# Attention and a gated MLP on one core: shared tile as column tiles, V loaded a group ahead, four scaled-activation buffers, a wider spread of the second batch's transposes, and later padding copies

## The chip, the cores and the metric

The kernel runs on one core of a Trainium2 chip. The metric is the device time of one execution in microseconds (us). Most numbers below come from one profiled execution of each kernel. TensorE is called PE, VectorE DVE, ScalarE ACT, GpSimd POOL and SyncE SP in the profile; SP and POOL issue most of the DMAs.

One measure of my own is used throughout. The kernel has a set-up and then nine feed-forward groups. **Groups** means the time from the start of the first feed-forward matmul (bank<-UT,W) to the end of the last VectorE instruction, and a group's length is the time between two such starts, read from the timeline.

## The reference

```python
# attention: B=8, H=8, S=576, D=64; window 32, 8 global positions
scores = scale * q @ k.T ; masked outside the window except global rows/columns
attn = softmax(scores) ; x = (attn @ v) as (B, S, 512)
# gated MLP over tokens, then channels
a1 = alpha1 * x + beta1
u  = x + lam * einsum('ts,bsd->btd', w_tok, a1)          # token mix, 576 x 576
a2 = alpha2 * u + beta2
out = u + lam * (relu(a2 @ w_ch1) @ w_ch2)               # 512 -> 2048 -> 512
```

## The kernel before

Each batch of 576 tokens is four tiles of 128 tokens and 64 left over; two batches share one tile for their leftovers ("S"). The feed-forward runs over nine groups of four tiles. While group g runs on PE, the attention of batch g+1, its token mix, and the loads of batch g+2 are woven in between by slot number (128 feed-forward matmuls make 128 slots). The program issues every engine's work in the order of the slots, so a slot number also fixes who stands behind whom in each queue.

```python
def finish_u(t, ps):                       # after a token-mix tile
    nc.vector.tensor_tensor(out=x, in0=ps, in1=x, op=ALU.add)           # DVE add, frees the bank
    ...
    ub = UB[nub[0] % 2]                    # two buffers
    nc.gpsimd.tensor_tensor(out=ub, in0=x, in1=A2, op=ALU.mult)         # POOL, 1.28 us
    nc.sync.dma_start_transpose(out=UT[g % 2][:, :, js], in_=ub)        # SP, UT feeds the next group

def tok_shared(p):                         # shared tile: 2 x 5 matmuls 128x512
    # par 0: columns 64:192 of wtT, par 1: columns 0:128; 64 of the 128 columns are zeros
    ...
def tr_pair(b, hp):                        # first two batches: transposes on PE
    ring = tr0_ps if b == 0 else sc_ps     # second batch: the two score banks
    ...
for g in range(9):                         # group g; nb = g + 2
    timed(prefetch(nb), slots, 1, 50)      # K, Q and V of batch nb
    timed(xbars(nb), slots, 44, 78)        # DMA transposes of K and Q; V's shifted copy
    timed([qpad(hp) ...] + [gcols(nb)], slots, 86, 104)   # DVE: padded copy QP<-QT
    ...                                    # gathered rows' transposes (KGT) at slots 56 and 60
    parts = [(attention(g + 1), 2, 83), (token_mix(g + 1), 97, 115 if g < 3 else 122)]
```

The softmax here doesn't subtract the row's maximum and nothing guards it: scores larger than these inputs give would overflow.

## Time and profile before

| | before |
|---|---|
| median of 3 runs | 419.55 us |
| profiled span | 418.4 us |
| first group starts at | 56.85 us |
| groups | 358.28 us |
| PE busy | 91% |

The head of the page (busy time, share of the span, instructions), the slice rows of PE and of its granted clock, and the chain that ended last:

```profile
PE 382.3 (91%) x3071; PEld 213.9 (51%) x3071; DVE 235.1 (56%) x621; ACT 168.3 (40%) x318; POOL 213.3 (51%) x285
PE   0658888998999989989999999999999999999996
PEclk9996899999999999999999999999999999999999
PE 65%; DVE 13%; DMA 11%; POOL 4%; issue 3%; ACT 2%; SPq 1%; DVEq 0%; POOLq 0%; ACTq 0%
```

PE is the limit, but not everywhere: the first five slices (52 us) are set-up, and later slices that are not 9 hold waits. The view of waits names them (who waited for whom; us in total, times, longest):

```profile
PE bank L117 <- DVE QP L567: 1.9, 2, 1.0
PE bank L117 <- DMA UT<-UB: 1.6, 2, 1.2
PE bank L117 <- POOL XL L397: 1.3, 1, 1.3
PE bank L117 <- DVE KGT L241: 1.2, 2, 0.9
PE bank L117 <- DVE XR L410: 1.2, 1, 1.2
...
PE bank L117 <- issue: 0.6, 1, 0.6
...
POOL UB L425 <- DMA UT<-UB: 11.1, 9, 2.3
...
DVE QP L214 <- issue: 4.4, 2, 2.8
```

The 0.6 us under "issue" are the wait at the start of the second group. A displayed wait is about 0.15 us shorter than the lost time, since the end of the matmul before it is modelled (that same wait is 0.72 us by the starts of the matmuls); from the starts of all matmuls the holes after the first group's start sum to 11.4 us. L117 is the line of the helper that issues nearly all matmuls, so tile names and not lines tell them apart.

### The profile page before, as it was taken

To read this page: it belongs to the slowest core of one execution; us is meant where nothing else is said; L and a number is where in the kernel's file an instruction comes from. 1 tells how busy PE (TensorE), PEld (TensorE's weight loads), DVE (VectorE), ACT (ScalarE), POOL (GpSimd) and SP (SyncE) were. 2 spreads that over 40 slices of the span, in tenths; PEclk is the share of its full clock that TensorE was granted. 3 is DMA by queue.
4 is the path that set the end of the run, shared out by engine and by line. 5 is a ranking of instruction groups with operands and counts; after the bars stand their busy time and mean duration, and the time that the engine had idled before them with its cause. 6 is when DMAs were issued, how large, how long until landed. Compare 5 with 4: busy or idle time off the path is not lost.

```text
span 418.4 us, 8079 instructions
## 1 busy us (share of the span) xinstructions
PE 382.3 (91%) x3071; PEld 213.9 (51%) x3071; DVE 235.1 (56%) x621; ACT 168.3 (40%) x318; POOL 213.3 (51%) x285
## 2 busy tenths in 40 slices
PE   0658888998999989989999999999999999999996
PEld 0538545653465446535664565456645654444443
DVE  3765495587355946586459556845577555104013
ACT  2545236810484057303840483038405820450720
POOL 8635938435865389427853797369514335100000
PEclk9996899999999999999999999999999999999999
DMA  8999999991999179946994499549963002201002
GB/s 179 246 239 223 115 178 112 144 121 50 132 155 150 64 120 128 146 101 102 164 144 111 102 137 145 119 92 152 137 132 101 0 15 76 75 2 75 25 27 76
DMA packets 161691, 48.26 MB, mean 115 GB/s; under 512 B 147530, under 2 KB 154770, under 8 KB 161652
## 3 DMA queue, kind: packets, MB, share of 16 engines
q0 software_dynamic: 98752, 16.99, 62.0%
q1 hardware_dynamic: 62100, 30.36, 38.8%
q8 instruction: 24, 0.39, 0.4%
q10 hardware_dynamic: 800, 0.39, 0.4%
q14 instruction: 15, 0.12, 0.1%
HBM read 39.28 MB, written 9.44 MB: 116 GB/s over the span
## 4 chain that ended last, share of the span: by engine, by line
PE 65%; DVE 13%; DMA 11%; POOL 4%; issue 3%; ACT 2%; SPq 1%; DVEq 0%; POOLq 0%; ACTq 0%
PE bank L117 64%; DMA XR<-in_q_dram 4%; DVE QP L214 3%; DMA Kb<-in_k_dram 2%; DMA QT<-Qb 2%; DVE QP L567 1%; DMA UT<-UB 1%; DMA SR<-in_k_dram 1%; DVE XR L507 1%; DVE OT L506 1%; POOL UB L425 1%; DVE XR L410 1%; DVE XR L353 1%; POOL XL L371 1%; ACT E L293 1%
## 5 line engine op out<-in xcount | busy, mean ns | idle before, releaser
L117 PE MATMUL bank<-UT,W 128*128 128x512 bf16 x576 | 159.8, 379 | 3.0 <-DMA UT<-UB 1.6
L117 PE MATMUL bank<-W,HT 128*128 128x512 bf16 (+2 forms) x592 | 140.4, 373 | 0.0
L491 ACT ACTIVATE HT<-bank,bias 128x512 bf16<-128x512 f32 x144 | 99.0, 687 | 68.3 <-PE bank L117 67.5
L293 ACT ACTIVATE E<-bank 128x416 f16<-128x416 f32 (+1 forms) x96 | 47.5, 514 | 130.7 <-PE bank L117 129.2
L117 PEld LDWEIGHTS <-HT 128*128 128x128 bf16 x592 | 53.7, 98 | 53.5 <-issue 0.4
L117 PEld LDWEIGHTS <-W 128*128 128x128 bf16 x640 | 50.2, 97 | 28.8 <-issue 3.7
L371 POOL TENSOR_TENSOR XL<-XR,LA 128x384 bf16<-128x384 f32 x32 | 32.3, 1010 | 63.2 <-DVE XR L353 38.3
L425 POOL TENSOR_TENSOR UB<-XR,A 128x512 bf16<-128x512 f32 x28 | 35.9, 1286 | 49.0 <-DVE XR L410 21.4
L506 DVE TENSOR_TENSOR OT<-bank,LAM 128x512 f32<-128x512 f32 (+2 forms) x37 | 24.9, 672 | 53.5 <-PE bank L117 53.3
L117 PE MATMUL bank<-XL,wtT 128*128 128x512 bf16 x180 | 46.8, 389 | 3.2 <-POOL XL L397 1.3
L117 PE MATMUL bank<-RG,G 128*128 128x65 f16 x320 | 44.4, 196 | 4.7 <-DVE RG L321 3.5
L117 PEld LDWEIGHTS <-PT 128*128 128x128 f16 x576 | 34.0, 100 | 21.6 <-issue 5.4
L117 PE MATMUL bank<-Ve,PT 128*128 128x65 f16 x320 | 44.5, 197 | 0.0
L117 PE MATMUL bank<-QP,KT 128*128 128x144 bf16 (+1 forms) x288 | 33.9, 232 | 6.2 <-ACT E L293 4.0
L117 PEld LDWEIGHTS <-G 128*128 128x128 f16 x320 | 31.6, 99 | 15.0 <-DVE G L248 0.2
L117 PEld LDWEIGHTS <-KT 128*128 128x128 bf16 x288 | 25.2, 102 | 23.6 <-issue 7.2
L117 PE MATMUL bank<-Vo,PT 128*128 128x65 f16 x256 | 36.1, 195 | 0.0
L198 POOL DMA_DIRECT2D Ve<-in_v_dram x40 | 34.4, 869 | 2.2 <-PE bank L117 0.9
L300 DVE TENSOR_TENSOR PGQ<-E,gqm 128x80 f16<-128x80 f16 x64 | 11.1, 215 | 36.7 <-ACT E L293 36.7
L117 PEld LDWEIGHTS <-wtT 128*128 128x128 bf16 x180 | 17.9, 99 | 23.9 <-issue 4.2
L353 DVE TENSOR_TENSOR XR<-bank,rd 128x384 f32<-128x384 f32 x64 | 27.2, 424 | 2.3
L507 DVE TENSOR_TENSOR XR<-OT,XR 128x512 f32<-128x512 f32 (+2 forms) x33 | 26.7, 810 | 1.6
(130 smaller groups left out, 413.1 us busy)
## 6 DMA issues: line engine op xcount, KB each, us to landing
out_dram<-XR SPq DMA_DIRECT2D x31, 256.0 KB, 2.3
W<-in_moe_w_ch_dram POOLq DMA_DIRECT2D x4, 1024.0 KB, 19.0
Vo<-Ve SPq DMA_DIRECT2D x14, 260.0 KB, 3.5
Ve<-in_v_dram POOLq DMA_DIRECT2D x24, 128.0 KB, 10.0
Kb<-in_k_dram POOLq DMA_DIRECT2D x24, 128.0 KB, 6.0
Qb<-in_q_dram POOLq DMA_DIRECT2D x24, 128.0 KB, 6.7
Ve<-in_v_dram POOLq DMA_DIRECT2D x16, 96.0 KB, 8.9
XR<-in_k_dram SPq DMA_DIRECT2D x3, 512.0 KB, 15.2
```

The lines of the kernel that those rows point to most:

```text
L117: nc.tensor.matmul(out=o, lhsT=l, rhs=r, start=st, stop=sp, skip_group_check=True)
L198: nc.gpsimd.dma_start(out=Ve[b % 2][r0 : r0 + hi - lo, c, :, 0:D], in_=v[b, :, lo:hi, :].rearrange("h p d -> p h d"))
L214: nc.vector.tensor_copy(out=QP[r, hp, a, :, 0:64], in_=QT[r, hp, 0:S].rearrange("p (t j) -> p t j", j=64))
L293: nc.scalar.activation(out=e[:, UOFF[u] : UOFF[u + 1]], in_=ps[:, 0:off], func=AF.Exp, bias=0.0, scale=0.125)
L300: nc.vector.tensor_tensor(out=pg[:, :, c0 : c0 + 16].rearrange("p c (a g) -> p c a g", a=2), in0=gq_in, in1=gq_m, op=ALU.mult)
L353: nc.vector.tensor_tensor(out=xo, in0=pv[:, :, :, 0:64], in1=rb, op=ALU.mult)
L371: xl_eng(b).tensor_tensor(out=XL[b % 2][:, 0:3, 128 * hp : 128 * hp + 128], in0=xo, in1=bass.AP(l.tensor, l.offset, [l.ap[0], [0, 3], [1, ...
L410: nc.vector.tensor_tensor(out=x, in0=ps, in1=x, op=ALU.add)
L425: nc.gpsimd.tensor_tensor(out=ub, in0=x, in1=A2, op=ALU.mult)
L491: nc.scalar.activation(out=HT[:, ec, :], in_=st["ps"], func=AF.Relu, bias=bias1[:, ec : ec + 1], scale=1.0)
L506: nc.vector.tensor_tensor(out=ot, in0=ps, in1=LAM[:, lo:hi], op=ALU.mult)
L507: nc.vector.tensor_tensor(out=x, in0=ot, in1=x, op=ALU.add)
```

## The change

Its intent: fewer PE slots for the shared tile, and fewer waits of PE at the second batch's transposes, at group starts and behind VectorE. The core of the diff (layout changes of wtT and set-up fills cut):

```diff
-    UB = [T(f"UB{i}", [P, DM], BF16) for i in range(2)]
+    UBt = T("UB", [P, 4, DM], BF16)
+    UB = [UBt[:, i, :] for i in range(4)]
...
     def tok_shared(p):
-        (two halves of five full-width matmuls)
+        def f():
+            ps = pv_ps()
+            for s in range(5):
+                for par in range(2):
+                    l = wt4o[:, 0:64] if s == 4 and par == 1 else wtT[:, s, 0:64]
+                    mm(ps[64 * par : 64 * par + 64, :], l, XL4[par] if s == 4 else XL[par][:, s, :], s == 0, s == 4)
+            finish_u(("S", p), ps)
...
-            ring = tr0_ps if b == 0 else sc_ps
+            ring = tr0_ps if b == 0 else pv_ps
...                                          (and their order among the scores)
-            timed(prefetch(nb), slots, 1, 50)                     # K, Q, V
+            timed(prefetch(nb), slots, 1, 34)                     # K, Q (first group: 1, 42, with V)
-            timed(xbars(nb), slots, 44, 78)
+            timed(xbars(nb), slots, 44, 75); V's copy at slot 78
-                slots[56], slots[60]: gathered rows' transposes
+                slots[84 if g else 98], slots[87 if g else 100]
-            timed([qpad...] + [gcols], slots, 86, 104)
+            timed([qpad...] + [gcols], slots, 89 if g else 101, 105 if g else 122)
+            timed(prefetch_v(nb + 1), slots, 85 if g else 122, 96 if g else 127)
-            parts = [(first_attention(1), 4, 98), (token_mix(1), 106, 120)]
+            parts = [(first_attention(1), 4, 94), (token_mix(1), 106, 119)]
```

More of the change, by code (lines that the diff above doesn't have):

```diff
@@ L153 @@
     W2 = T("W2", [P, 16, DM], BF16)
-    wtT = T("wtT", [P, 5, 704], BF16)
-    wt4o = T("wt4o", [P, 704], BF16)
+    wtT = T("wtT", [P, 5, S], BF16)
+    wt4o = T("wt4o", [P, S], BF16)
     mask = T("mask", [P, NW, 64], FP16)
@@ L182 @@
     TST = SR[:, 1, :]
-    WTB = HTt[:, 0 : 5 * 640].rearrange("p (c s) -> p c s", c=5)
+    WTB = HTt[:, 0 : 5 * S].rearrange("p (c s) -> p c s", c=5)
     def xs(t):
@@ L422, in finish_u @@
             return
-        ub = UB[nub[0] % 2]
+        ub = UB[nub[0] % 4]
         nub[0] += 1
@@ L432, in f @@
             ps = pv_ps()
-            cs = slice(192 + 128 * i, 320 + 128 * i)
+            cs = slice(64 + 128 * i, 192 + 128 * i)
             for s in range(4):
@@ L441, in tok_shared @@
     def tok_shared(p):
-        st = {}
-        def half(par):
-            def f():
-                if par == 0:
-                    st["ps"] = pv_ps()
-                ps = st["ps"]
-                cs = slice(64, 192) if par == 0 else slice(0, 128)
-                for s in range(4):
-                    mm(ps, wtT[:, s, cs], XL[par][:, s, :], par == 0 and s == 0, False)
-                mm(ps, wtT[:, 4, cs] if par == 0 else wt4o[:, cs], XL4[par], False, par == 1)
-                if par == 1:
-                    finish_u(("S", p), ps)
-            return (1.1, f)
-        return [half(0), half(1)]
+        def f():
[5 more added lines that the diff above has]
+            finish_u(("S", p), ps)
+        return [(1.1, f)]
     def gap(w):
@@ L527 @@
     OT = [OTt[:, 0:DM], OTt[:, DM : 2 * DM]]
-    LB = T("LB", [P, DM], FP32)
+    LB = UBt[:, 2:4, :].rearrange("p a b -> p (a b)").bitcast(FP32)
     def fill(ap, val=0.0, eng=None):
@@ L644 @@
     fill(Ve[0][:, :, :, 64:65], 1.0, g_)
-    fill(WTB[:, :, S:640], 0.0, g_)
-    fill(WTB[64:128, 4, :].bitcast(FP32), 0.0, g_)
     for hp in range(HP):
@@ L680 @@
     fill(G[:, :, 640:704], 0.0, g_)
-    fill(wtT[:, :, 0:64], 0.0, g_)
     fill(wt4o[0:64, :].bitcast(FP32), 0.0, g_)
-    fill(wt4o[64:128, 0:64], 0.0, g_)
+    fill(wtT[64:128, 4, :].bitcast(FP32), 0.0, g_)
     fill(ones, 1.0, g_)
@@ L730, in wtok_tr @@
         ps = mlp_ps().bitcast(BF16)
-        cols = slice(128 * k, 128 * k + 128) if k < 5 else slice(448, 576)
-        for n, tcn in enumerate((4, 0, 1, 2, 3)):
-            nc.tensor.transpose(out=ps[:, 128 * n : 128 * n + 128], in_=WTB[:, tcn, cols], identity=identb)
+        c0, n = (128 * k, 128 if k < 4 else 64) if k < 5 else (448, 128)
+        cols = slice(c0, c0 + n)
+        nc.tensor.transpose(out=ps[0:n, 0:64], in_=WTB[0:64, 4, cols], identity=identb[0:64, 0:64])
+        for t in range(4):
+            nc.tensor.transpose(out=ps[0:n, 64 + 128 * t : 192 + 128 * t], in_=WTB[:, t, cols], identity=identb)
         if k < 5:
-            nc.scalar.copy(out=wtT[:, k, 64:704], in_=ps[:, 0:640])
+            nc.scalar.copy(out=wtT[0:n, k, :], in_=ps[0:n, 0:S])
         else:
-            nc.scalar.copy(out=wt4o[64:128, 64:704], in_=ps[64:128, 0:640])
+            nc.scalar.copy(out=wt4o[64:128, :], in_=ps[64:128, 0:S])
     def run(*items):
@@ L780 @@
     for sc_ in range(5):
-        mm(psr, ones, wtT[:, sc_, 192:704], sc_ == 0, sc_ == 4)
+        mm(psr, ones, wtT[:, sc_, 64:576], sc_ == 0, sc_ == 4)
     for sc_ in range(5):
-        mm(psr2[:, 0:64], ones, wtT[:, sc_, 64:128], sc_ == 0, sc_ == 4)
-    nc.scalar.copy(out=wtT[64:65, 4, 192:704], in_=psr[64:65, :])
-    nc.scalar.copy(out=wtT[64:65, 4, 64:128], in_=psr2[64:65, 0:64])
-    nc.scalar.copy(out=wt4o[0:1, 192:704], in_=psr[0:1, :])
-    nc.scalar.copy(out=wt4o[0:1, 64:128], in_=psr2[0:1, 0:64])
+        mm(psr2[:, 0:64], ones, wtT[:, sc_, 0:64], sc_ == 0, sc_ == 4)
+    nc.scalar.copy(out=wtT[64:65, 4, 64:576], in_=psr[64:65, :])
+    nc.scalar.copy(out=wtT[64:65, 4, 0:64], in_=psr2[64:65, 0:64])
+    nc.scalar.copy(out=wt4o[0:1, 64:576], in_=psr[0:1, :])
+    nc.scalar.copy(out=wt4o[0:1, 0:64], in_=psr2[0:1, 0:64])
     psb = mlp_ps()
@@ L810, in first_attention @@
         w = [pv_x(b, hp) + pv_y(b, hp) for hp in range(HP)]
-        a = [t_[0], tr_tail(b), gap(0.3), g[0], t_[1], gap(0.3), g[1], gap(0.3)] + s[0] + [t_[2], gap(0.3), g[2], s[1][0], s[1][1], t_[3], gap(0.3), g[3], s[1][2], gap(0.5)]
+        a = [t_[0], tr_tail(b), gap(0.5), t_[1], g[0], gap(0.5), g[1], gap(0.3), s[0][0], t_[2], gap(0.3), s[0][1], g[2], s[0][2], t_[3], gap(0.3)]
+        a += [s[1][0], g[3], s[1][1], s[1][2], gap(0.4)]
         a += [gk_all(b, pv_ps), gap(0.5), q_[0], gap(0.6), s[2][0], s[2][1]] + w[0] + [q_[1], s[2][2], s[3][0], s[3][1]] + w[1] + [q_[2], s[3][2], gap(0.9)]
@@ L821, in prefetch, with prefetch_v @@
             a.append(lambda c=c: load_kq_std(q, Qb, b, c))
-        for c in range(5):
-            a.append(lambda c=c: load_v(b, c))
-        return a
+        return a
+    def prefetch_v(b):
+        return [lambda c=c: load_v(b, c) for c in range(5)]
     def xbars(b):
@@ L830, in xbars @@
             a.append(lambda c=c: xbar_q(b, c))
-        a.append(lambda: copy_vo(b))
         return a
@@ L848 @@
         if nb < NB:
+            if g == 0:
+                timed(prefetch(nb) + prefetch_v(nb), slots, 1, 42)
+            else:
+                timed(prefetch(nb), slots, 1, 34)
+            timed(xbars(nb), slots, 44, 75)
+            slots[78].append(lambda: copy_vo(nb))
             if nb % 2 == 0:
                 pr = nb // 2
-                slots[1].append(lambda pr=pr: gather(pr))
+                slots[1].insert(0, lambda pr=pr: gather(pr))
                 slots[44] += [lambda: gather_x(0), lambda: gather_x(1)]
-                slots[56].append(lambda pr=pr: gather_tr(pr, 0))
-                slots[60].append(lambda pr=pr: gather_tr(pr, 1))
-            timed(prefetch(nb), slots, 1, 50)
-            timed(xbars(nb), slots, 44, 78)
-            timed([lambda hp=hp: qpad(hp) for hp in range(HP)] + [lambda: gcols(nb)], slots, 86, 104)
+                slots[84 if g else 98].append(lambda pr=pr: gather_tr(pr, 0))
+                slots[87 if g else 100].append(lambda pr=pr: gather_tr(pr, 1))
+            timed([lambda hp=hp: qpad(hp) for hp in range(HP)] + [lambda: gcols(nb)], slots, 89 if g else 101, 105 if g else 122)
+            if nb + 1 < NB:
+                timed(prefetch_v(nb + 1), slots, 85 if g else 122, 96 if g else 127)
         def wrap(i):
```

## The prediction

> **What bounds it now.** The page's engine table has TensorE (PE) busy 91% of a 418.4 us span; no other engine passes 56%, and the chain of waits gives PE 65%. The slice row shows two regimes: set-up until about 57 us, with PE fed slowly by DMA, VectorE and ScalarE, then nine groups in which PE is nearly full. From 57 us only two things can shorten the run: fewer PE slots, or fewer holes between them. I listed the starts of all matmuls in the PE timeline (a 128x512 one starts every 0.2145 us) and summed what exceeds that pace after 57 us: about 11 us, in few places:
>
> - 60 to 70 us, second batch's transposes: 3.3 us (VectorE copies of QP, then ScalarE's exponential)
> - 96 to 98 us: 1.8 us (POOL's XL, behind VectorE's QP padding)
> - group starts at 109, 150, 234 us: 0.7, 1.4, 0.6 us (UB to UT)
> - 171 and 255 us: 0.5 and 1.0 us (copy of the gathered transposes, KGT)
> - 184 us: 1.3 us (VectorE held until the QT transposes landed)
>
> **What the change does.**
>
> 1. Column tiles. A shared tile is ten 128x512 matmuls, 2.15 us. It becomes five pairs whose 64-column halves use different array columns. The Trainium skill, "TensorE: Matmul & The Clock Gate", Part 3, says such matmuls run concurrently; "TensorEngine Tiling (Array Packing)", Key Properties and Restrictions, says that a change of mode drains the array and that column tiling has no fast weight load. No pair is in this trace. I expect 1.3 to 1.4 us instead of 2.15: 0.75 us, four times, 3 us, all on PE's path.
> 2. Second batch's transposes in three PV banks, interleaved with scores: removes the wait for two score banks. But VectorE has about 9.8 us of copies and masks in a stretch where PE has 7.4 us, so not all goes: 2 us of 3.3.
> 3. First group: QP padding after the last norms. The 1.8 us hole goes, but padding now meets the token-mix adds (0.69 us each) and output adds; VectorE is near full from slot 93 on, so the wait at the next group start grows. Net 1.3 us.
> 4. V a group ahead: a third of the loads leaves the stretch where K/Q loads and QT/KT transposes (7.8 us to landing) run. The VectorE wait for QT (2.8 us) and the 184 us hole go: 1.2 us.
> 5. Four UB: POOL's 11.1 us of waits on UT<-UB mostly vanish; on PE's path 1 us at group starts.
> 6. Gather transposes later: 1.5 us at 171 and 255.
> 7. Set-up: fewer fills (0.9 us POOL), shorter copies of wtT: at most 0.3 us on the path.
>
> Sum about 10 us, less some 2 us for new waits: V loads just before the token mix may slow UT landings (2.5 us median, 6.0 at worst), and VectorE queues.
>
> **Prediction.** 411.3 us, range 407.8 to 415.0; faster by over 2%: 0.47; within 2%: 0.51; slower: 0.02.
>
> **What would show it.** Shared-tile matmuls start in pairs a few ns apart, five pairs in about 1.1 us plus switches; gk in the first group starts about 2 us earlier relative to the group's start; no PE wait on KGT; PE waits on UT<-UB under 1 us in total; POOL's wait on UT<-UB below 3 us; no VectorE wait for QT; PE holes after 57 us about 4 us instead of 11.
>
> **What would make it wrong.** The tiles do not overlap (weight loads serialise them): 3 us lost. VectorE is so full between 60 and 70 us, or at the end of the first group, that holes only move. V traffic delays UT, so that each group start gains a wait. All good together would give about 407.

## The result, and the profile after

The changed kernel took 406.65 us at the median (405.53 to 408.16, 4 runs) beside 419.52 us for the kernel before; the ratio is 0.9698 (95% interval 0.9657 to 0.9739). Ratios here are the mean time of one kernel's fast runs over that of the other's of the same rounds, so not quite the ratio of the medians. 406.65 lies 1.2 us under the stated range, and the gain of 12.9 us is more than one and a half times the 8.2 us predicted.

The same parts of the page, after:

```profile
PE 375.4 (93%) x3071; PEld 210.2 (52%) x3071; DVE 230.0 (57%) x621; ACT 167.2 (41%) x318; POOL 210.5 (52%) x282
PE   0657889999899999999999999999999999999996
PEclk9998999999999999999999999999999999999999
PE 87%; DVE 6%; POOL 2%; DMA 1%; issue 1%; ACT 1%; SPq 0%; DVEq 0%; POOLq 0%
```

Its waits, those of PE from the first group's start on (the view of waits with a window from 54.8 us): of the first five PE lines shown of before only two small rests stand, both on QP; line numbers moved by a few.

```profile
PE bank L117 <- issue: 1.1, 1, 1.1
...
PE bank L556 <- DVE QP L560: 0.4, 1, 0.4
PE bank L117 <- DVE QP L560: 0.3, 1, 0.3
...
POOL UB L426 <- DMA UT<-UB: 0.3, 1, 0.3
```

The 1.1 us under "issue" are the wait at the start of the second group, for UT. VectorE no longer waits for QT at all. The profiled spans are 418.4 and 403.6 us, 14.8 us apart. They split into groups (358.28 to 345.91, 12.37 us), first group's start (56.85 to 54.87, 1.98 us) and the end after the last VectorE instruction (3.28 to 2.87 us, 0.41 us, which no run here explains). The 1.98 us cannot be put down to the change: over the profiles of all twenty kernels below the first group starts anywhere from 54.65 to 57.61 us, and the kernel before with small additions is found at 54.93, 56.19 and 56.58. So the groups are what has to be explained. Their lengths, in us:

| group | 1 | 2 | 3 | 4 | 5 | 6 | 7 | 8 | 9 | sum |
|---|---|---|---|---|---|---|---|---|---|---|
| before | 52.37 | 40.98 | 43.82 | 40.17 | 42.99 | 39.89 | 41.76 | 27.63 | 28.66 | 358.28 |
| after | 47.63 | 39.61 | 41.13 | 39.61 | 41.13 | 39.61 | 40.91 | 27.63 | 28.65 | 345.91 |

The shared tile itself, in the PE timeline of the kernel before (start us, us, engine, line, operation, operands, array shape, count); its ten matmuls are the rows on XL:

```profile
103.54 1.24 PE L117 MATMUL bank<-XL,wtT 128*128 128x512 bf16 x5
104.62 0.59 PE L117 MATMUL bank<-W,HT 128*128 128x512 bf16 x2
105.05 1.03 PE L117 MATMUL bank<-XL,wtT 128*128 128x512 bf16 x4
105.92 0.38 PE L117 MATMUL bank<-XL,wt4o 128*128 128x512 bf16 x1
```

and after:

```profile
96.68 0.81 PE L117 MATMUL bank<-W,HT 128*128 128x512 bf16 x3
97.42 1.27 PE L117 MATMUL bank<-XL,wtT 128*64 128x512 bf16 x9
98.31 0.38 PE L117 MATMUL bank<-XL,wt4o 128*64 128x512 bf16 x1
98.62 0.60 PE L117 MATMUL bank<-W,HT 128*128 128x512 bf16 x2
```

Ten full-width matmuls take ten slots of 0.2157 us. The column tiles take 1.20 us from the first start (97.42) to the next ordinary matmul (98.62), and 0.1 us more on the way in: the third of the matmuls at 96.68 starts at 97.11, so 0.31 us pass and not 0.2157. A tile thus costs 1.3 in place of 2.16 us and saves 0.86 us.

### The profile page after: what moved, and what is told of

Read it like the earlier page. It is cut to its first block, busy times and chain, and to the rows that moved or that the text cites. A ratio compares the mean times of both kernels' runs of the same rounds, so it can differ in the third digit from the quotient of the medians.

```text
span 403.6 us, 8090 instructions
## 1 busy us (share of the span) xinstructions
PE 375.4 (93%) x3071; PEld 210.2 (52%) x3071; DVE 230.0 (57%) x621; ACT 167.2 (41%) x318; POOL 210.5 (52%) x282
## 4 chain that ended last, share of the span: by engine, by line
PE 87%; DVE 6%; POOL 2%; DMA 1%; issue 1%; ACT 1%; SPq 0%; DVEq 0%; POOLq 0%
PE bank L117 86%; DMA SR<-in_k_dram 1%; DVE QP L560 1%; POOL XL L372 1%; PE bank L556 0%; POOL Ve L199 0%; PE bank L418 0%; DVE PT L306 0%; DVE OT L539 0%; POOL XL L717 0%; DVE PT L525 0%; ACT QP L560 0%; DVE QP L576 0%; DVE Kb L539 0%; ACT E L294 0%
## 5 line engine op out<-in xcount | busy, mean ns | idle before, releaser
L117 PE MATMUL bank<-XL,wtT 128*128 128x512 bf16 (+1 forms) x180 | 41.2, 380 | 0.5 <-POOL XL L372 0.5
L301 DVE TENSOR_TENSOR PGQ<-E,gqm 128x80 f16<-128x80 f16 x64 | 10.2, 201 | 34.5 <-ACT E L294 32.7
L192 POOL DMA_DIRECT2D Kb<-in_k_dram x30 | 26.8, 894 | 0.1
```

The source lines that it names most:

```text
L117: nc.tensor.matmul(out=o, lhsT=l, rhs=r, start=st, stop=sp, skip_group_check=True)
L192: nc.gpsimd.dma_start(out=dst[0:n, c, :].rearrange("p (h d) -> p h d", d=D), in_=src[b, :, c * P : c * P + n, :].rearrange("h p d -> p h d"))
L301: nc.vector.tensor_tensor(out=pg[:, :, c0 : c0 + 16].rearrange("p c (a g) -> p c a g", a=2), in0=gq_in, in1=gq_m, op=ALU.mult)
```

## The experiments

Eighteen kernels ran; each was timed beside the kernel before on the same chip. Labels with a_ start from the changed kernel, those with b_ from the kernel before.

### Is a column tile fast because two run side by side?

a_unpaired:

```diff
-            for s in range(5):
-                for par in range(2):
+            for par in range(2):
+                for s in range(5):
```

> The changed kernel, with the ten column-tile matmuls of a shared tile in another order: five of the lower half, then five of the upper, so that neighbours are in the same half. Same instructions, same weights, same operands. Theory (the saving is two matmuls running side by side): a shared tile goes back from 1.20 us to about 2.1 us, 3.6 us more in all from the first group on (348.7 to about 352.3 us from the first feed-forward matmul to the end). Rival (a 64-column matmul is cheap for itself): still about 1.2 us a tile, no change.

Measured: groups 346.66 us (+0.75), 407.89 us at the median. Neither theory as I wrote it: the tile took 1.44 us, from 98.57 to 100.01:

```profile
98.57 1.30 PE L117 MATMUL bank<-XL,wtT 128*64 128x512 bf16 x9
99.70 0.38 PE L117 MATMUL bank<-XL,wt4o 128*64 128x512 bf16 x1
100.01 0.82 PE L117 MATMUL bank<-W,HT 128*128 128x512 bf16 x3
```

In program order, five matmuls in the lower half need 4 x 0.2157 = 0.86 us before the fifth starts, and the last of the upper five could not start before 1.7 us. It starts after 1.13 us. The single records show the same: the second and third matmul to start do so at 98.806 and 98.811 us, 5 ns apart, although the first five of the program are all of the lower half. (That the compiler had put them in another order is unlikely: the records' semaphore counts fall on the third, fourth and fifth of one stream of five, as in the kernel before, and not on every second matmul, as in the changed kernel.) So either 64-column matmuls are cheap, or the hardware lets upper ones start beside lower ones that stand before them. The next run decides.

a_samehalf puts all ten into the lower half (the upper 64 tokens of the shared tile then get a wrong token mix):

```diff
-                    mm(ps[64 * par : 64 * par + 64, :], l, ..., s == 0, s == 4)
+                    mm(ps[0:64, :], l, ..., s == 0 and par == 0, s == 4 and par == 1)
```

> Wrong result on purpose: the changed kernel with all ten 64-column matmuls of a shared tile in the lower half of the array. In the run with the order changed the tile still took 1.44 us, so the order is not what makes it fast. Theory (halves run side by side, and the hardware finds the pairs by itself): with one half only, nothing can run beside, and a tile takes about 2.15 us again. Rival (a 64-column matmul takes half the time for itself): 1.2 to 1.5 us.

```profile
98.52 2.13 PE L117 MATMUL bank<-XL,wtT 128*64 128x512 bf16 x9
100.48 0.38 PE L117 MATMUL bank<-XL,wt4o 128*64 128x512 bf16 x1
100.80 1.47 PE L117 MATMUL bank<-W,HT 128*128 128x512 bf16 x6
```

A tile takes 2.28 us (98.52 to 100.80), groups 349.56 us (+3.65), and the matmuls of one half start 0.216 us apart. Side by side it is, and the pairs form without alternating order, which is only 0.24 us a tile better. The Trainium skill, "TensorE: Matmul & The Clock Gate", Part 3, is right that tiles in different columns run concurrently; its sentence there that matmuls keep program order does not fit a_unpaired. (The result passed the check although the token mix of all shared tiles was wrong: it enters with lam, drawn at about 0.01, so this check would not catch such an error.)

### What do column tiles and UB buffers give alone?

b_coltile is the kernel before with the new tok_shared alone, on the old layout of wtT (columns 64:128), weight and slots unchanged.

> The kernel before, with only the shared tile as alternating column tiles; its slots in the schedule unchanged. Theory: the 0.95 us a tile come off PE's path one for one, 3.8 us in all (361.6 to about 357.8 us from the first feed-forward matmul to the end). Rival: the saved slots only bring the group start forward into a longer wait for UB to UT, so under 2.5 us.

Measured: groups 357.58 us (-0.70), ratio 0.998. The rival held. The shared tiles did take 1.2 us, but the waits grew; the kernel before showed 1.6 us for UT<-UB, 1.2 for XR and 0.6 for issue on these lines:

```profile
PE bank L117 <- issue: 2.5, 4, 1.4
PE bank L117 <- DMA UT<-UB: 2.1, 2, 1.2
PE bank L117 <- DVE XR L410: 1.9, 2, 1.2
PE bank L117 <- DVE KGT L241: 1.4, 2, 1.1
```

b_ub4 is the kernel before with four UB (and the beta row sharing their space, as in the change):

```diff
-        ub = UB[nub[0] % 2]
+        ub = UB[nub[0] % 4]
```

> The kernel before with four UB buffers, nothing else. With two buffers in the changed kernel the groups took 3.2 us longer (349.1 against 345.9 us from the first feed-forward matmul to the last VectorE instruction). If a part's worth is the same wherever it stands: 358.3 falls to about 355. If it depends on the rest (my theory now: PE has only one chain of VectorE, POOL and DMA at a group's start to wait for, and before that chain was held by other links too): about 1 to 2 us.

Measured: groups 354.94 us (-3.34), ratio 0.9952. It was the other branch: the full worth, not 1 to 2 us. PE's wait on UT<-UB fell only from 1.6 to 1.0 us. By group, the first six became shorter by 0.56, 0.53, 1.34, 0.07, 0.55 and 0.29 us. The largest single gain is in the third group (43.82 to 42.48): its hole at 184 us is gone, and VectorE no longer waits for QT there, with V loaded as before. POOL, free of its waits on UT<-UB, issued that group's first K load 1.9 us sooner (93.9 in place of 95.8 us after the first group's start).

b_ub4_ct has both.

> The kernel before with four UB buffers and column tiles. Column tiles alone gave 0.7 us, not the 3.8 us that PE saves, since the waits for UB to UT and for VectorE grew by 3.1 us. Theory (the saved slots are paid out only once UB and UT no longer limit the group starts): the two together give clearly more than the sum of the two alone, 4 us or more. Rival (additive): the sum.

Measured: groups 353.79 us (-4.49), ratio 0.9896. The sum of the two alone is 4.04 us, so they help each other by 0.45 us. That misses "clearly more": with four UB the column tiles still pay only 1.15 of their 3.4 us. VectorE's wait for QT came back (1.2 and 1.1 us), and with it 0.8 us of the hole at 184 us: PE had become faster, and the loads had not.

a_ub2 takes two of the four buffers away from the changed kernel (`% 4` back to `% 2`).

> The changed kernel with two UB buffers instead of four, all else kept. Theory (four buffers free the group starts): the waits at the starts of the second, third and fifth group come back, 1 to 2 us in all; POOL waits some 9 us in total for UT<-UB again. Rival (those waits went because V loads no longer sit in the way): under 0.5 us.

```profile
PE bank L117 <- issue: 2.5, 4, 1.6
PE bank L117 <- DMA UT<-UB: 1.9, 1, 1.9
```

Groups 349.12 us (+3.21), against 1 to 2 us expected; POOL's waits on UT<-UB came back at 9.6 us in total, as expected. The second group took 41.64 in place of 39.61 us (+2.03), the third 0.64 and the first 0.53 us more. The wait at the fifth group's start, expected back too, did not come: the fourth group kept its 39.61 us.

### The parts of the schedule, each taken back from the changed kernel

a_trsc: the second batch's transposes back in the score banks and in the old order.

```diff
-            ring = tr0_ps if b == 0 else pv_ps
+            ring = tr0_ps if b == 0 else sc_ps      # and the order of first_attention as before
```

> The changed kernel with the second batch's transposes back in the two score banks and in the order of before. Theory: the holes of 60 to 70 us of the kernel before (3.3 us) come back where 1.2 us are left, so the first group takes 2.1 us longer (47.6 to about 49.7 us) and nothing else changes.

Measured: first group 49.86 us (+2.23), all others the same to 0.01 us. As expected.

a_vold: V again with K and Q.

```diff
-            timed(prefetch(nb), slots, 1, 34)
+            timed(prefetch(nb) + prefetch_v(nb), slots, 1, 50)
-                timed(prefetch_v(nb + 1), slots, 85, 96)
```

> The changed kernel with V loaded in the same group as K and Q, as before, spread over slots 1 to 50; V's copy and all else kept. Theory (V ahead removed the 1.3 us hole in the third group, where VectorE waited for QT): VectorE waits for QT again and PE has about 1.3 us more of holes. Rival (four UB and earlier K/Q already give that): under 0.4 us.

Measured: groups 346.43 us (+0.52). VectorE's wait for QT came back with 0.8 and 0.3 us and QT landed after 8.0 us in place of 6.4, but PE lost only 0.5 us. Nearer the rival: with four UB the late V costs little. Nor does the hole come back in a_ub2, which has V ahead and two UB. In the changed kernel either remedy may be missing, then; but four UB are not enough in every setting, since with column tiles alone beside them (b_ub4_ct) most of the hole was there.

a_gtr_early: gathered rows' transposes at slots 56 and 60 again, from the second group on.

> The changed kernel with the gathered rows' transposes back at slots 56 and 60 of the second, fourth (and every even-batch) group. Theory (their bank waits behind VectorE's copy and takes a PV bank from the attention): PE waits on KGT's copy come back, 0.5 us at about 170 and 1.0 us at 255, so the groups take about 1.4 us longer (345.9 to 347.3 us). Rival (only a symptom of a VectorE that was late for another reason): under 0.4 us.

Measured: groups 346.55 us (+0.64), half of what was expected, 0.32 us in each of two groups. So the place of these transposes explains less than half of the KGT wait of before (1.52 us by the starts of the matmuls). In b_ub4, where they stood at the old slots, its larger part fell from 1.01 to 0.46 us.

a_qpad86: the padding QP<-QT three slots earlier, from the second group on.

```diff
-    ... slots, 89 if g else 101, 105 if g else 122)
+    ... slots, 86 if g else 101, 104 if g else 122)
```

> The changed kernel with the QP padding of the groups from the second on in slots 86 to 104 in place of 89 to 105. Theory (padding ahead of the token-mix adds in VectorE's queue holds the adds and, with them, UB and UT): the groups take 1 to 3 us longer from the second on, as holes on UT or on the adds. Rival (three slots are nothing once V is out of the way): under 0.3 us.

```profile
PE bank L117 <- issue: 1.4, 3, 1.1
PE bank L117 <- DMA UT<-UB: 1.1, 2, 0.7
```

Measured: groups 347.54 us (+1.63): +0.84, +0.25 and +0.56 us in the second to fourth group. Three slots, 0.65 us of feed-forward matmuls, are worth more than the V loads and the gathered transposes together. The fourth group is back at exactly the 40.17 us of the kernel before, and its whole gain of 0.56 us is thus the padding's: two UB left it at 39.61 us (a_ub2). The theory holds, that padding ahead of the token-mix adds in VectorE's queue holds the adds, POOL's UB and the UT transpose: the lost time is again a wait for UT at the group starts.

a_qpad_old: the first group's padding back at slots 86 to 104, with its gathered transposes at 56 and 60.

> The changed kernel with the QP padding of the first group back in slots 86 to 104 (with its gathered transposes at 56 and 60, which it needs). Theory (padding stood in VectorE's queue ahead of the last norms): the first group takes 1.2 us longer (47.6 to 48.8 us), with the hole on XL back and the wait at the second group's start shorter by 0.4 us. Rival (the earlier end of the attention, slot 94 in place of 98, was enough): under 0.4 us.

Measured: groups 350.98 us (+5.07), first group 49.84 (+2.21) and second 42.46 (+2.85). The hole on XL did not come back at all (no wait on XL stands after set-up), so for that hole the rest of the change, the attention's end at slot 94 in place of 98 among it, was enough. But the wait for UT at the second group's start grew from 1.1 to 3.3 us, where I had expected it to shrink. The PE timeline there:

```profile
105.81 1.01 PE L117 MATMUL bank<-UT,W 128*128 128x512 bf16 x2 [3.29 <-issue]
106.62 0.56 PE L117 MATMUL bank<-QP,KT 128*128 128x144 bf16 x3
106.96 0.63 PE L117 MATMUL bank<-UT,W 128*128 128x512 bf16 x1
```

Two things meet. The add of the first token-mix tile came after all the padding, so POOL made four UB back to back, and SP's queue put an output store ahead of the last UT transpose (issued at 101.86 us). V's loads for the batch after next began at 102.30 us; the wait ended 3.95 us after that issue, against 2.6 us in the changed kernel. That the V loads slowed it is likely, not shown. (The one UT transpose of the changed kernel's first group that was issued beside V's loads, at 101.55 us, also took 4.0 us to land; in the kernel before, the one at 108.6 us beside K's and Q's loads took 4.5 us.) From 104.8 to 111.7 us, beginning in that wait, PE's granted clock was 0.5: the windows view (us; busy of PE, PEld, DVE, ACT, POOL; granted clock, DMA share, GB/s) gives

```profile
104.00:106.00 2.00, 0.19 (x1) 0.14 (x2) 0.00 (x0) 0.00 (x0) 2.00 (x4) 0.71 1.76 134
106.00:108.00 2.00, 2.00 (x10) 1.14 (x9) 0.00 (x0) 0.55 (x2) 2.00 (x3) 0.50 2.21 175
108.00:110.00 2.00, 2.00 (x8) 0.95 (x7) 0.00 (x0) 1.43 (x3) 2.00 (x4) 0.50 2.18 175
110.00:112.00 2.00, 2.00 (x8) 0.99 (x7) 1.05 (x4) 1.03 (x3) 2.00 (x4) 0.59 2.44 153
```

The Trainium skill, "TensorE: Matmul & The Clock Gate", says to allow no idle gaps over about 3 us between matmul bursts, and this agrees: a 3.3 us wait cost the second group 2.85 us more. Waits up to 1.9 us at a group's start (a_ub2) cost no such thing. But not every execution pays it whole: the profiled one (mean granted clock 0.978, 411.71 us) has some 18 us at half clock, while two of the other three (409.54 and 408.27 us) have a mean of 0.992, which leaves about 6.5 us in all, and every profile here spends at least 3.4 of them in set-up. So 2.2 us of the 5.07 are the waiting itself, and 2.85 us came on top in the execution that was profiled.

### Set-up

a_warm1 starts 32 matmuls on constant data at 1.5 us, while PE waits for loads; a_warm2 adds ten at 29.7 us.

```diff
+    fill(UT[0][:, 0, :], 0.5)
+    spin(banks[3], 32)                  # matmuls UT[0] x UT[0] into a bank not yet in use
...
-    run(gq[0], gq[1], pv[0], ...
+    run(gq[0], gq[1], act(spin, banks[0], 10), pv[0], ...      # a_warm2 only
```

> An attempt to beat both: the changed kernel with 32 matmuls on constant data (no result used) while PE waits for the first loads, 1 to 10 us. All runs so far show matmuls of set-up at half pace (a 128x512 matmul 0.43 us apart) for one or two stretches of 3.4 us between 31 and 51 us, and time from the token mix to the first group either 7.65 or 9.33 us. Theory (PE's pace in set-up depends on its own busy time before): the first global-key matmuls (16 in 3.9 us at 24 us) take about 2 us, and the first group starts 1 to 4 us earlier. Rival (set-up waits for loads and VectorE, and PE's idle stretches of 10 to 24 us cool it again): no change over 0.5 us.

> As the last, with ten more such matmuls where PE waits 2.7 us for VectorE at 29 us. Theory: PE stays at full pace from there, the half-pace stretches at 31 to 38 us and 48 to 51 us vanish in every run, the token mix to the first group takes 7.65 us each time, and the first group starts 2 to 4 us earlier than in the changed kernel's median. Rival: if PE is at half pace there, ten take 4.3 us and delay PE by 1.7 us.

Measured: first token mix at 47.49 and 47.14 us, first group at 56.81 and 56.07 us, 406.69 and 406.62 us at the median. No gain. The 16 global-key matmuls at 24.5 us still took 4.04 us in a_warm2: PE's pace had fallen again. a_warm2 did remove the half-pace stretch after its spin, and the first token mix still began where it always did. So PE's pace up to there is not what set-up waits for. The one place where it shows is the token mix of the first batch: from there to the first group, eighteen of the twenty profiles take 7.65 us, or 9.33 us when a half-pace stretch falls on it (a_best took 8.49 and a_warm2 8.93 us) (before, the windows view gives a clock of 0.55 and 0.60 from 48 to 52 us; the changed kernel's profile has 1.00). The four executions of the changed kernel fall into two pairs, with mean granted clocks of 0.996 and 0.987 and spans some 2 us apart, so one kernel can get either; I found no way to choose it.

a_setup moves W2's loads and two V chunks behind the last XL products in POOL's queue and the 64 small bias matmuls ahead of the last PV product.

> An attempt to beat both: the changed kernel with set-up's order changed: the loads of W2 and of the last V chunks issued after the last XL products in POOL's queue, the 64 small bias matmuls before the last PV product, the columns of alpha2 and beta2 transposed early. Theory (POOL's queue and PE's small matmuls stand before the first token mix): the first token mix starts at about 45.9 us in place of 46.6 to 48.3, 1 to 1.5 us gained in every run. Rival (set-up waits for loads): no change.

Measured: first token mix at 47.05 us, no gain; and the V chunks now came too late, with a new line in PE's waits and a half-pace stretch behind it, so the first group took 51.73 us. 408.87 us at the median, where a_tm101 had 406.33 us in the same session.

```profile
PE bank L117 <- DMA Vo<-Ve: 2.5, 1, 2.5
```

### Can the last wait go?

a_tm101: the first group's token mix at slots 101 to 114 in place of 106 to 119, its padding at 104 to 126.

> An attempt to beat both: the changed kernel with the first group's token mix at slots 101 to 114 in place of 106 to 119, and its padding at 104 to 126 in place of 101 to 122. Theory (the wait of 1.1 us for UT at the second group's start is the chain add, UB, UT of the last tile it needs, begun too late): the wait goes and the first group takes 46.3 to 46.8 us in place of 47.6. Rival (VectorE is the limit there, so the order of its work only moves the wait): no gain, or a wait on XL or QP in its place.

Measured: first group 46.35 us (-1.28) as the theory has it, but second 40.56 (+0.95): PE waited 0.8 us for the last piece of the padding, the global columns of QP (L227), which now came too late. The wait had moved in part; 406.33 us at the median.

a_best is a_setup and a_tm101 together.

> Both of the last two. If they do not meet: the sum of their gains, about 2.3 us less than the changed kernel, 404 to 405 us at the median.

Measured: groups 345.58 us, first token mix at 48.13 us, 406.83 us at the median: a_tm101's gain, and nothing from set-up. The 404 to 405 us expected were missed. (V's late chunks happened to arrive in time in its profile.)

a_pads1 keeps the early token mix and makes the global columns second instead of last; a_pads2 makes the third and fourth pad in the second group.

```diff
-            parts = [(first_attention(1), 4, 94), (token_mix(1), 106, 119)]
+            parts = [(first_attention(1), 4, 94), (token_mix(1), 101, 114)]
+            pads = [pads[0], lambda: gcols(nb)] + pads[1:] if g == 0 else ...   # at 101 to 124
```

> The changed kernel with the first group's token mix at slots 101 to 114 and its padding in the order first pad, global columns, other three pads, at 101 to 124. Theory (VectorE's order, not its load, makes the waits): both the wait on UT and the one on the global columns go, the first group takes 46.4 us and the second 39.6: groups 344.6 us in place of 345.9. Rival (VectorE is full): the wait appears in another place and the groups stay at 345.5 to 346.

> As the last, but the third and fourth pad are made in the second group (slots 6 and 10), so that VectorE has 1.8 us less before the group's start. Both theories: first group 46.4, second 39.6, groups 344.6 us; if only this one gets there, VectorE's load was the limit.

Measured: groups 344.64 us in both, first group 46.35 and second 39.61 us, exactly the sum expected. a_pads1 moves no work out of the group and gains as much as a_pads2, so VectorE's order was the limit here, not its load. Holes of over 0.25 us after the first group's start are down to the two of the second batch's transposes (0.4 and 0.3 us). At the median 406.05 and 405.87 us, ratios 0.9638 (0.9605 to 0.9670) and 0.9654 (0.9620 to 0.9689) to the kernel before. The groups are 1.27 us shorter than in the changed kernel; in whole times that is within the spread that set-up makes, and the two were not timed beside the changed kernel.

## Why the prediction was wrong

The direction and nearly every place were right; the sum was too small, some causes do not stand as given, and one part of the change had no term. The prediction's own "all good together would give about 407" is nearly what came. Set against the lengths of the groups, the terms of the prediction read as follows (measured values from the group table, with the terms of one group separated by the holes in the PE timeline):

| step, as predicted | predicted us | measured us |
|---|---|---|
| 1 column tiles | 3.0 | 3.4 (4 x 0.86) |
| 2 transposes of the second batch | 2.0 | 2.2 (a_trsc) |
| 3 first group, padding, net | 1.3 | 1.65 (group 1: 4.74 less 0.86 and 2.23; holds some 0.5 of four UB) |
| 4 the hole at 184 us (group 3) | 1.2 | 1.3 |
| 5 group starts (put down to four UB) | 1.0 | 1.9 (groups 2 and 4: 1.37 and 0.56) |
| 6 the holes on KGT (gathered transposes) | 1.5 | 1.5 |
| small holes not listed | 0 | 0.3 |
| new waits | -2.0 | 0 |
| sum over the groups | 8.0 | 12.4 |

- **The step that failed is "less some 2 us for new waits".** V's loads just before the token mix were to slow UT, and VectorE's queue was to make new holes. UT landed after 2.5 us at the median before and after (at worst 6.0 and 4.2), and from the second group on PE had no wait for UT left. The wait at the second group's start did grow, from 0.6 to 1.1 us, but that was already in step 3's net. The allowance was taken twice and without a place for it. It is nearly half of the miss. The fear itself was not groundless: in a_qpad_old, where UT was a little later, the wait became 3.3 us.
- **Padding in the later groups had no term, and its gain stands in the table under step 5.** The starts of the third and fifth group gained 1.9 us. Four UB added to the kernel before shorten the two groups ahead of them by only 0.53 and 0.07 us (b_ub4); taking back the three slots of padding costs them 0.84 and 0.56 us (a_qpad86). In sum that is 0.6 us for four UB and 1.4 us for the padding, which is a third of the miss. (In the second group both are needed: two UB cost it 2.03 us in a_ub2.)
- **Step 5 itself had the right size and missed most of what four UB do.** The 1 us was for three group starts, where b_ub4 gives 0.56, 0.53 and 0.07 us, 1.16 in sum. But four UB gave 3.34 us in the kernel before and are worth 3.21 us in the changed one. The rest lies where the prediction had other causes: 1.34 us in the third group (step 4), 0.55 us in the fifth (step 6) and 0.29 us in the sixth. POOL's 11.1 us of waits also held back loads, as the K load 1.9 us sooner in b_ub4 shows.
- **Step 1 was a little low**: 0.75 us a tile predicted, 0.86 measured. Overlap, a price for the change of mode (0.1 us on each side) and the five pairs were as predicted. So was the global-key step of the first group, 2.3 us sooner after the group's start.
- **Step 4 had the right size and a cause that is only one of two.** V ahead was to remove the wait for QT. Four UB alone remove it too (b_ub4), though not beside column tiles (b_ub4_ct), and it stays away with V ahead and two UB (a_ub2); from the changed kernel, V's early loads are worth 0.5 us. That the size came out right is partly luck.
- **Step 3 had nearly the right net and the wrong cause.** Padding was to free XL, at the price of a longer wait at the next group's start. With the padding back at its old slots (a_qpad_old) XL is not late, and that wait is 2.2 us longer, not shorter. So the later padding shortens the wait for UT, and for XL the rest of the change, with the attention's earlier end, is enough. In one execution the long wait also halved PE's pace, which made it 5.07 us.
- **Step 6 had the right size and half of its cause.** Both holes went, but from the changed kernel the later transposes are worth 0.64 us (a_gtr_early).
- **Step 7, set-up (0.3 us)**: the runs neither show nor exclude it; set-up varies by 3 us. The profiled execution after was a lucky one (403.6 us; the slower pair of its four executions had spans near 406 us).
- **"PE holes after 57 us about 4 us instead of 11"**: 2.5 us remain.

A sum of terms also hid something that the runs show. Column tiles alone give 0.70 us, yet taking the pairing from the changed kernel costs 3.65 us. PE's saved slots are paid out only if the add, UB and UT of the next group come earlier by as much. Four UB beside them are not enough for that (1.15 of 3.4 us, b_ub4_ct); that the schedule, with the place of the padding in VectorE's queue (1.63 us for three slots), does the rest is argued from a_qpad86, not shown by adding it. The single worths from the changed kernel's side (3.65, 3.21, 2.23, 5.07, 1.63, 0.64 and 0.52 us) add up to 17 us and not to 12.4. The 2.85 us of half pace in a_qpad_old account for part of this; that several of them hold the same chain is the likely reason for the rest.

What stays open: which of the remaining parts pays out how much of the column tiles (no run adds the schedule to the kernel before without UB and column tiles), what decides set-up's 3 us, and whether V's loads were the reason for the slow UT landing in a_qpad_old.

## What to carry to other kernels

When PE is the limit but stands at a handover in every round, slots saved on PE alone turn into waits: cost the chain behind the handover (here add, scale, transpose) in the same step, and value a part both by adding it to the old kernel and by taking it from the new one. Look at the order in an engine's queue before its load: keeping copies three slots later, out of the way of the adds that release the next round, was worth 1.6 us here, and moving the first group's token mix and copies gave another 1.3 us. Give every part of a change its own term, also one that looks like mere tuning. Write down allowances for new waits only with a place and a number for each.

## What the Trainium skill lacked or had wrong

- "TensorE: Matmul & The Clock Gate", Part 3, has matmuls strictly in program order. With five lower-half matmuls ahead of five upper-half ones, the ten started within 1.13 us and not the 1.7 us or more that program order needs (a_unpaired), and the tile took 1.44 us; all in one half took 2.28 us. The same part's sentence that weight loads overlap running matmuls only where the row group differs does not fit either (its paragraph on the mechanism allows more, through the background weight buffer): from the third on the ten loads of a shared tile, all on the same rows, run under its matmuls, which start in pairs every 0.216 us.
- "TensorEngine Tiling (Array Packing)", Key Properties, says that a change of mode drains the array, without a price. Here it is 0.1 us on the way in and 0.1 us on the way out (starts 0.31 us apart in place of 0.2157).
- The same page, Restrictions, has column tiling without fast weight load. The trace agrees, and the page lacks the number: a load of 64 columns takes 106 to 110 ns in the shared tile, where one of 128 columns takes 97 ns in the ordinary mode.
- "TensorE: Matmul & The Clock Gate" ties half pace to idle gaps of some 3 us and, in "A second HAM failure mode", to frequent short ones, for which it has no figure. The half-pace stretch from 48 us in the kernel before follows PE idle times of at most 0.7 us; between them lay many small matmuls (64 of one column each). No page says how such matmuls count as activity, and 42 matmuls put into set-up (a_warm2) did not prevent it. Whether the short idle times or the small matmuls bring it about is not shown.
